# Attention scores of 16-bit batches: K's halves stacked over 128 rows, one head at a time

## The chip, the cores and the metric

The kernel runs on one core of one Trainium2 chip. A core has four compute engines with instruction streams of their own: TensorE (PE; its weight loads stand in the profile as PEld), VectorE (DVE), ScalarE (ACT) and GpSimd (POOL). SyncE (SP) issues the DMA transfers. The metric is device microseconds of one execution; before the change the median of three runs is 1104.53 us (1103.01 to 1106.8).

## What is computed

Eight batches, eight heads, 576 positions, head size 64: attention in a window of 128 positions with a linear bias, then a transform over positions and features, a norm and a two-layer network of width 2048.

```python
scores = scale * np.matmul(q, k.transpose(0, 1, 3, 2))
scores = np.where(mask, scores + bias[None], -1000000000.0)   # 0 <= rel < 128
attn = softmax(scores); attn_out = np.matmul(attn, v)
X = np.fft.fft(np.fft.fft(x, axis=1), axis=2); u = x + np.real(X)
un = (u - mean) / np.sqrt(var + 1e-06)
return u + np.maximum(un @ w_ch1, 0.0) @ w_ch2
```

## The kernel before, in words

**Pairs and tiles.** Two heads of a batch form a pair; pair p is batch p // 4 and heads 2j, 2j + 1 with j = p % 4. Q and K lie in memory with the head size over partitions, head 2j on partitions 0 to 63 and head 2j + 1 on 64 to 127. The queries of a head are cut into five tiles (`TILES`), four of 128 queries and one of 96; tile 0 sees 128 keys, the others 256. `SGRP` puts the tiles into three groups for the scores: (1, 0), (3, 2) and (4).

**Two kinds of batch.** Batches 0 to 2 (`NF = 3`) compute the scores in 32-bit numbers, one product per tile and head. Batches 3 to 7 split each 32-bit operand into a 16-bit high part and a 16-bit rest: `convert` (L331) makes the high part by an ACT copy (L353) and the rest by a DVE subtraction (L354, in the profile as L158). Q and K of a pair are converted whole, on 128 partitions, and V in the same way. `scores` (L362) then makes, for each tile and each head, three products over the 64 rows of that head: high by high, rest by high, high by rest (`prods`, L368), all added up in PSUM. The inner loop runs over the two heads, so that the products of the two heads alternate, each with its own PSUM tile, sp0 or sp1 (two buffers each).

**After the scores.** L390 reduces the scores with the bias and writes them to P; an exponential follows on ACT, then `halves` (L397) splits P into two 16-bit parts (ACT L403 and DVE), `flip` transposes them by DMA into pt (L412), and `values` (L428) multiplies them with V's two parts (L445 to L447). `weigh` (L451) divides by the sums and writes the batch's X.

**The rest of a batch.** `fourier` (L493) does the transform, `norm` (L647) the norm with transposes by DMA into uT, and `ffn` (L685) the two layers: L698 fills a PSUM tile fp with 24 products of 256 columns (or 48 of 128), ACT (L703) and DVE evacuate it into hbuf, and L712 makes the second layer from hbuf, 48 products of 512 columns per tile. Two PSUM buffers serve fp. Of the transform, 64 rows of every two batches are left over; they are gathered in a tile `ut` (L500, two buffers) and go through the network by themselves, with uT in a spare half of the second layer's weight tile (L653).

**What sets the order.** Every step is put into a heap with a time by hand (`put`), and the steps are emitted in the order of these times; from batch 1 on a batch has 24 units of time and a pair 6. A pair that starts at t loads Q and K at t - 7 (`load`, L301), converts Q at t - 4.6 and K at t - 3.6 (L733), makes the scores of its three groups at t, t + 2 and t + 4, both heads together (L736), and the value products at t + 5.66 to t + 10.66, head by head, one unit apart (L740). Loads, DMA transposes and outputs all go out from SP's queue, in order, and each waits there until its buffer is free. The framework then adds the semaphores and may move an instruction ahead on its engine when a modelled timeline has room for it. Buffers: one each for the raw Q (qr) and the raw K (kr), two each for the converted Q (qq) and K (kk).

`batch_scales` (L244) reads Q, K and V of a coming 16-bit batch through two slots (fetches at L253) and squares them on ACT (L257) to find the scales, among them `nsl`, whose columns 8 to 11 hold Q's scale by pair.

Of the kernel before, what the change touches and what calls it, by code (L numbers as in the profile page):

```python
# [76 lines left out]
def attn_fft_ffn_kernel(  # L77
# [30 lines left out]
    slope_sb = const.tile([128, 16], F32, name="slope_sb")  # L108
# [135 lines left out]
    def batch_scales(b, t0, dt):  # L244
# [19 lines left out]
        def scale():  # L264
# [8 lines left out]
            nsl = small.tile([128, 12], F32, name="nsl")  # L273
            V.tensor_scalar(nsl[:, 0:8], slope_sb[:, 0:8], gi[:, 0:1], None, ALU.mult)
            V.tensor_scalar(nsl[:, 8:12], slope_sb[:, 8:12], sc[:, 0:1], None, ALU.mult)
# [25 lines left out]
    def load(p):  # L301
        b, j = divmod(p, 4)
        qr = att.tile([128, NQ], F32, name="qr", bufs=1)
        if b < NF:
            kr = att.tile([128, 2, NQ], F16, name="kk").rearrange("p e t -> p (e t)").bitcast(F32)[:, 0:NK]
        else:
            kr = att.tile([128, NK], F32, name="kr", bufs=1)
        nc.sync.dma_start(out=qr, in_=q[b, j])
        nc.sync.dma_start(out=kr, in_=k[b, j])
        raws[p] = [qr, kr]  # L310

# [19 lines left out]
    def convert(p, what):  # L331
        b, j = divmod(p, 4)
        if b < NF:
            qr, kr = raws[p]
            qs = att.tile([128, 2, NQ], F16, name="qq").rearrange("p e t -> p (e t)").bitcast(F32)
# [4 lines left out]
        if what < 2:  # L340
            pair = att.tile([128, 2, NQ], F16, name="qk"[what] * 2)
            n, s = ((NQ, nsl[:, 8 + j:9 + j]), (NK, sc[:, 1:2]))[what]
            hi, lo, src = pair[:, 0, 0:n], pair[:, 1, 0:n], raws[p][what]
            ops.setdefault(p, []).extend((hi, lo))
        else:
# [6 lines left out]
            ops[p] += vh, vl  # L352
# [9 lines left out]
    def scores(p, i):  # L362
        b, j = divmod(p, 4)
        if b < NF:
            prods = ((ops[p][0], ops[p][1]),)
        else:
            qh, ql, kh, kl = ops[p][:4]
            prods = ((qh, kh), (ql, kh), (qh, kl))  # L368
        grp = SGRP[i]
        sp = [ps_s.tile([128, 512], F32, name=f"sp{e}") for e in range(2)]  # L370
        col = 0
        for ti in grp:
            c0, m, blks = TILES[ti]
            n = 128 * len(blks)
            for x, (qq, kk) in enumerate(prods):
                for e in range(2):
                    h = slice(64 * e, 64 * e + 64)
                    T.matmul(sp[e][:m, col:col + n], qq[h, c0:c0 + m], keys(kk[h], ti),  # L378
                             start=(x == 0), stop=(x == len(prods) - 1))
            col += n  # L380
        P = Ps[p, i] = {}
        for e in range(2):
# [45 lines left out]
    def values(p, i, e):  # L428
# [5 lines left out]
        for ti in TGRP[i]:  # L434
            m, blks = TILES[ti][1:]
            n = len(blks)
            for x, (vc, _) in enumerate(blks):
# [5 lines left out]
                vh, vl = ops[p][4:]  # L443
# [49 lines left out]
    def fourier(b, t0):  # L493
        st = {}

        def begin():
            XA = Xs[b]
            st["X"], st["X2"], st["sc"] = [XA[:, i] for i in XS], XA[:, 2], scs[b][0]
            if b % 2 == 0:
                uts[b // 2] = xp.tile([128, DM], F32, name="ut", bufs=2)  # L500
# [370 lines left out]
```

## Time and profile before

| | |
|---|---|
| runs | 1106.8, 1104.53, 1103.01 us |
| profiled execution | 1103.87 us |
| its span | 1102.1 us |
| mean granted clock of TensorE | 0.978 |
| PE / DVE / ACT busy | 1069.7 / 688.5 / 566.9 us |
| 16-bit score products (L378) | from 290.97 us (start of the first) to 899.24 us (last run of them) |

Busy times are sums over the whole span and say nothing of a stage. A row of a timeline gives the start, the length and, after an x, how many instructions stand in it. Matmuls are pipelined: the length of one is its latency, and the distance between two starts is the room that it takes. In a row of waits stand the total in us, the times and the longest. In a form such as `64*128 64x256 f16` the first product is rows by columns of the weights, the second partitions by columns of the data that stream through.

### The profile page before, as it was taken

The numbers are of one execution on the slowest core, as the hardware profiler recorded it, in microseconds if no ns is written. First come the engines' busy times: TensorE is split into PE (matmuls) and PEld (weight loads), VectorE is DVE, ScalarE is ACT, GpSimd is POOL, SyncE is SP. The second block draws the span as 40 slices with busy tenths as digits, with TensorE's granted clock in tenths as the row PEclk, the third lists the DMA queues.
The fourth block names the chain that finished last, engine by engine and source line by source line (L and its number), as shares of the span: only waits on it lengthen the run. The fifth ranks groups of instructions, "written<-read, shape, count | busy, mean of one in ns | idle before, by whom it ended". The sixth has DMA issues, their size and how long they took to land.

```text
span 1102.1 us, 23512 instructions
## 1 busy us (share of the span) xinstructions
PE 1069.7 (97%) x9220; PEld 754.4 (68%) x9220; DVE 688.5 (62%) x2023; ACT 566.9 (51%) x1333; POOL 20.1 (2%) x58
## 2 busy tenths in 40 slices
PE   6989999999888999999999999999999999999998
PEld 5777778686755666676667677585857676757665
DVE  6989678137456586868767585868685755262111
ACT  5867688448746565457534474456544441241000
POOL 0000000000000000000000000001000000010000
PEclk9989869999989999999999999999999999999999
DMA  9951245414656455344633144334531230030000
GB/s 368 321 191 57 66 109 162 129 35 104 200 155 146 131 100 109 76 102 83 129 80 85 42 106 100 86 81 105 119 86 37 56 81 1 20 53 16 20 10 20
DMA packets 170655, 109.61 MB, mean 99 GB/s; under 512 B 135472, under 2 KB 144944, under 8 KB 170544
## 3 DMA queue, kind: packets, MB, share of 16 engines
q1 hardware_dynamic: 169968, 106.66, 37.5%
q8 instruction: 72, 1.18, 0.4%
q10 hardware_dynamic: 576, 1.45, 0.3%
q14 instruction: 39, 0.32, 0.1%
HBM read 66.91 MB, written 9.44 MB: 69 GB/s over the span
## 4 chain that ended last, share of the span: by engine, by line
PE 83%; DMA 6%; DVE 5%; ACT 4%; issue 1%; SPq 0%; POOL 0%; ACTq 0%; DVEq 0%
PE fp L698 31%; PE fp L712 30%; PE sp L378 6%; PE pv L440 4%; PE pd L554 3%; DMA wall<-q_dram 2%; PE sp L421 2%; PE fp L299 2%; PE pd L588 1%; ACT wall L257 1%; DMA wall<-k_dram 1%; DMA vr<-v_dram 1%; PE pv L445 1%; ACT P L158 1%; PE pv L447 1%
## 5 line engine op out<-in xcount | busy, mean ns | idle before, releaser
L712 PE MATMUL fp<-wall,hbuf 128*128 128x512 f16 x1728 | 395.5, 381 | 2.9 <-DVE hbuf L158 2.9
L698 PEld LDWEIGHTS <-wall 128*128 128x128 f16 x3840 | 338.4, 98 | 53.2 <-issue 14.0
L698 PE MATMUL fp<-uT,wall 128*128 128x256 f16 x3072 | 361.1, 273 | 7.8 <-DVE hbuf L158 4.8
L712 PEld LDWEIGHTS <-hbuf 128*128 128x128 f16 x1728 | 163.3, 99 | 186.5 <-issue 10.0
L158 ACT ACTIVATE P<-P,nb 128x256 f32<-128x256 f32 x320 | 141.2, 478 | 117.3 <-DVE nb L390 117.2
L703 ACT ACTIVATE hbuf<-fp 128x512 f16<-128x512 f32 x144 | 85.0, 590 | 194.2 <-PE fp L698 194.2
L158 DVE SCALAR_TENSOR_TENSOR hbuf<-fp,hbuf 128x512 f16<-128x512 f32 x144 | 98.9, 688 | 136.1 <-ACT hbuf L703 135.5
L390 DVE CUSTOM_DVE_ANT_0 P<-sp,rg,nsl 128x256 f32<-128x256 f32 x200 | 80.5, 450 | 49.6 <-PE sp L378 49.5
L378 PE MATMUL sp<-kk,qq 64*128 64x256 f16 (+5 forms) x840 | 100.7, 310 | 6.8 <-DMA kk<-k_dram 5.4
L158 DVE SCALAR_TENSOR_TENSOR P<-P 128x256 f16<-128x256 f32 x200 | 73.5, 389 | 19.2 <-ACT P L403 17.9
L403 ACT ACTIVATE P<-P 128x256 f16<-128x256 f32 x200 | 70.9, 382 | 0.5 <-DMA pt<-P 0.3
L257 ACT ACTIVATE wall<-wall 128x512 f32<-128x512 f32 (+2 forms) x75 | 45.2, 604 | 48.1 <-DMA wall<-v_dram 20.3
L440 PEld LDWEIGHTS pv<-vr,pt 128*128 128x128 f32 x432 | 59.8, 213 | 4.6 <-issue 1.2
L440 PE MATMUL pv<-vr,pt 128*128 128x65 f32 x432 | 62.5, 294 | 0.2 <-DVE X L462 0.2
L158 DVE SCALAR_TENSOR_TENSOR X<-fp,misc,X 128x512 f32<-128x512 f32 x32 | 23.8, 743 | 56.3 <-PE fp L712 56.3
L390 DVE CUSTOM_DVE_ANT_0 P<-sp,rel_sb 128x256 f32<-128x256 f32 x120 | 42.1, 388 | 7.9 <-PE sp L378 7.9
L446 PE MATMUL pv<-vl,pt 128*128 128x64 f16 x360 | 46.4, 193 | 0.0
L447 PE MATMUL pv<-vhs,pt 128*128 128x65 f16 x360 | 46.3, 194 | 0.0
L445 PE MATMUL pv<-vhs,pt 128*128 128x65 f16 x360 | 45.9, 195 | 0.3 <-DVE X L462 0.3
L378 PEld LDWEIGHTS sp<-kk,qq 64*128 64x128 f32 (+1 forms) x240 | 31.9, 204 | 20.1 <-ACT qq L336 5.6
L698 PE MATMUL fp<-wall,wall 128*128 128x128 f16 x768 | 45.4, 219 | 0.1
L424 ACT ACTIVATE pt<-sp 128x384 f32<-128x384 f32 (+2 forms) x72 | 32.6, 464 | 15.7 <-PE sp L421 13.8
(146 smaller groups left out, 1197.7 us busy)
## 6 DMA issues: line engine op xcount, KB each, us to landing
qr<-q_dram SPq DMA_DIRECT2D x32, 304.0 KB, 3.0
hbuf<-w_dram SPq DMA_DIRECT2D x16, 512.0 KB, 6.7
out_dram<-X SPq DMA_DIRECT2D x32, 256.0 KB, 2.4
wall<-v_dram SPq DMA_DIRECT2D x25, 256.0 KB, 3.0
vr<-v_dram SPq DMA_DIRECT2D x20, 320.0 KB, 3.2
kr<-k_dram SPq DMA_DIRECT2D x20, 289.0 KB, 3.4
X<-w_dram SPq DMA_DIRECT2D x11, 512.0 KB, 5.3
wall<-q_dram SPq DMA_DIRECT2D x20, 256.0 KB, 2.8
```

The costliest lines, as they stand in the source:

```text
L158: put(now[0] + dt, lambda: f(*a, **kw))
L257: A.activation(t, t, AF.Square, accum_out=box["mx"][:, i, c:c + 1])
L378: T.matmul(sp[e][:m, col:col + n], qq[h, c0:c0 + m], keys(kk[h], ti), start=(x == 0), stop=(x == len(prods) - 1))
L390: V.tensor_tensor_reduce(pt[:m, 0:n], sp[e][:m, col:col + n], tab[:m, pc:pc + n], mul, 3.0e38, ALU.add, ALU.min, nb[:m, ti:ti + 1])
L403: A.activation(hi, P32, AF.Copy, scale=2.0 ** 14)
L440: T.matmul(pv[:, ti], pt[:, col:col + 128], ops[p][2][:, e, vc], start=first, stop=last)
L445: T.matmul(pv[:, ti], ph, vh[:, e, vc], start=first, stop=False)
L446: T.matmul(pv[:, ti, 0:D], ph, vl[:, e, vc], start=False, stop=False)
L447: T.matmul(pv[:, ti], pl, vh[:, e, vc], start=False, stop=last)
L698: T.matmul(fp[:, i * n:(i + 1) * n], w1_ap(e, c, f0 + i), uT[:, j, c, 0:n], start=(c == 0 and p == 0), stop=(c == 3 and p == 2))
L703: A.activation(ht[:, 0], fp, AF.Relu)
L712: T.matmul(op, hh[f][:, a, i * 128:(i + 1) * 128], w2_ap(e, f), start=(f == 0 and p == 0), stop=(f == 15 and p == 2))
```

## The change

In the 16-bit batches a head's scores no longer use its 64 rows of the array but all 128. K's high part and its rest are stacked over the partitions (head 0: high on 0 to 63 and rest on 64 to 127; head 1 the other way round), and Q of one head is loaded twice, onto both halves of the partitions. One product of Q's high part with the stack adds high by high and high by rest; a second one adds rest by high and rest by rest. So a tile takes two products per head, where there were three. The scores are made head by head: head 0 at t, t + 1, t + 2 and head 1 at t + 3, t + 4, t + 5.

Q is loaded and converted by head (loads at t - 7 and t - 4, conversions at t - 4.6 and t - 1.6), and K's two halves of 64 partitions are converted separately (t - 3.6 and t - 1.6). The pool of converted Q has three buffers, of which a pair takes two. To make room, `ut` has one buffer, and every second one of its tiles lies in the spare half of the second layer's weight tile. The table of slopes gets eight more columns, so that `nsl` holds Q's scale by head.

```diff
-            nsl = small.tile([128, 12], F32, name="nsl")
+            nsl = small.tile([128, 16], F32, name="nsl")
...
-            V.tensor_scalar(nsl[:, 8:12], slope_sb[:, 8:12], sc[:, 0:1], None, ALU.mult)
+            V.tensor_scalar(nsl[:, 8:16], slope_sb[:, 16:24], sc[:, 0:1], None, ALU.mult)
...
     def load(p):
         b, j = divmod(p, 4)
-        qr = att.tile([128, NQ], F32, name="qr", bufs=1)
         if b < NF:
+            qr = att.tile([128, NQ], F32, name="qr", bufs=1)
+            nc.sync.dma_start(out=qr, in_=q[b, j])
             kr = att.tile([128, 2, NQ], F16, name="kk").rearrange("p e t -> p (e t)").bitcast(F32)[:, 0:NK]
         else:
             kr = att.tile([128, NK], F32, name="kr", bufs=1)
-        nc.sync.dma_start(out=qr, in_=q[b, j])
+            qr = None
         nc.sync.dma_start(out=kr, in_=k[b, j])
         raws[p] = [qr, kr]
+
+    def load_q(p, e):
+        b, j = divmod(p, 4)
+        qr = raws[p][0] = att.tile([128, NQ], F32, name="qr", bufs=1)
+        nc.sync.dma_start(out=qr, in_=bass.AP(tensor=q.tensor, offset=q[b, j, 64 * e].offset,
+                                              ap=[[0, 2], [NQ, 64], [1, NQ]]))
...
-    def convert(p, what):
+    def convert(p, what, e=0):
...
-        if what < 2:
-            pair = att.tile([128, 2, NQ], F16, name="qk"[what] * 2)
-            n, s = ((NQ, nsl[:, 8 + j:9 + j]), (NK, sc[:, 1:2]))[what]
-            hi, lo, src = pair[:, 0, 0:n], pair[:, 1, 0:n], raws[p][what]
-            ops.setdefault(p, []).extend((hi, lo))
+        if what == 0:
+            s, src = nsl[:, 8 + 2 * j + e:9 + 2 * j + e], raws[p][0]
+            pair = ops.setdefault(p, {})["q", e] = att.tile([128, 2, NQ], F16, name="qq", bufs=3)
+            hi, lo = pair[:, 0], pair[:, 1]
+        elif what == 1:
+            if e == 0:
+                ops[p]["k"] = att.tile([128, 2, NQ], F16, name="kk")
+            own, other = slice(64 * e, 64 * e + 64), slice(64 - 64 * e, 128 - 64 * e)
+            s, src = sc[own, 1:2], raws[p][1][own]
+            hi, lo = (ops[p]["k"][x, e, 0:NK] for x in (own, other))
...
-    def scores(p, i):
+    def scores(p, i, heads=(0, 1)):
...
-        sp = [ps_s.tile([128, 512], F32, name=f"sp{e}") for e in range(2)]
+        sp = {e: ps_s.tile([128, 512], F32, name=f"sp{(e + (i if b >= NF else 0)) % 2}") for e in heads}
...
-            for x, (qq, kk) in enumerate(prods):
-                for e in range(2):
+            for e in heads:
+                if b < NF:
                     h = slice(64 * e, 64 * e + 64)
-                    T.matmul(sp[e][:m, col:col + n], qq[h, c0:c0 + m], keys(kk[h], ti),
-                             start=(x == 0), stop=(x == len(prods) - 1))
+                    T.matmul(sp[e][:m, col:col + n], ops[p][0][h, c0:c0 + m], keys(ops[p][1][h], ti),
+                             start=True, stop=True)
+                    continue
+                for x in range(2):
+                    T.matmul(sp[e][:m, col:col + n], ops[p]["q", e][:, x, c0:c0 + m], keys(ops[p]["k"][:, e], ti),
+                             start=(x == 0), stop=(x == 1))
...
-                uts[b // 2] = xp.tile([128, DM], F32, name="ut", bufs=2)
+                uts[b // 2] = wall[1][:, 8, 512:1024] if b // 2 % 2 else xp.tile([128, DM], F32, name="ut", bufs=1)
...
-            for what, x in enumerate((4.6, 3.6, -2 if early else 1.2)):
-                put(t - x, convert, p, what)
+            for e in range(2):
+                put(t + 3 * e - 7, load_q, p, e)
+                put(t + 3 * e - 4.6, convert, p, 0, e)
+                put(t + 2 * e - 3.6, convert, p, 1, e)
+            put(t - (-2 if early else 1.2), convert, p, 2)
         for i in range(3):
-            put(t + 2 * i * f, scores, p, i)
+            if b < NF:
+                put(t + 2 * i * f, scores, p, i)
+            else:
+                put(t + i, scores, p, i, (0, ))
+                put(t + i + 3, scores, p, i, (1, ))
```

More of the change, by code (lines that the diff above doesn't have):

```diff
@@ L107, in attn_fft_ffn_kernel @@
     rel_sb = const.tile([128, 1152], BF16, name="rel_sb")
-    slope_sb = const.tile([128, 16], F32, name="slope_sb")
+    slope_sb = const.tile([128, 24], F32, name="slope_sb")
     tab1_sb = const.tile([128, 4, 3, NS], F16, name="tab1_sb")
@@ L334, in convert @@
             qr, kr = raws[p]
-            qs = att.tile([128, 2, NQ], F16, name="qq").rearrange("p e t -> p (e t)").bitcast(F32)
+            qs = att.tile([128, 2, NQ], F16, name="qq", bufs=3).rearrange("p e t -> p (e t)").bitcast(F32)
             A.activation(qs, qr, AF.Copy, scale=slope_sb[:, 12 + j:13 + j])
@@ L351, in convert @@
             src = raws.pop(p)[2].rearrange("p a b c -> p (a b) c")
-            ops[p] += vh, vl
+            ops[p]["v"] = vh, vl
         A.activation(hi, src, AF.Copy, scale=s)
@@ L360, in keys @@
         return t[:, a0:a0 + 128 * len(TILES[ti][2])]
-    def scores(p, i):
+    def scores(p, i, heads=(0, 1)):
         b, j = divmod(p, 4)
[L364 to L368, printed above, removed]
         grp = SGRP[i]
-        sp = [ps_s.tile([128, 512], F32, name=f"sp{e}") for e in range(2)]
+        sp = {e: ps_s.tile([128, 512], F32, name=f"sp{(e + (i if b >= NF else 0)) % 2}") for e in heads}
         col = 0
@@ L374, in scores @@
             n = 128 * len(blks)
-            for x, (qq, kk) in enumerate(prods):
-                for e in range(2):
+            for e in heads:
+                if b < NF:
                     h = slice(64 * e, 64 * e + 64)
-                    T.matmul(sp[e][:m, col:col + n], qq[h, c0:c0 + m], keys(kk[h], ti),
-                             start=(x == 0), stop=(x == len(prods) - 1))
+                    T.matmul(sp[e][:m, col:col + n], ops[p][0][h, c0:c0 + m], keys(ops[p][1][h], ti),
[4 more added lines that the diff above has]
+                             start=(x == 0), stop=(x == 1))
             col += n
-        P = Ps[p, i] = {}
-        for e in range(2):
+        P = Ps.setdefault((p, i), {})
+        for e in heads:
             h = 2 * j + e
@@ L442, in values @@
                     continue
-                vh, vl = ops[p][4:]
+                vh, vl = ops[p]["v"]
                 ph, pl = (pt[:, o:o + 128] for o in (POUT[ti] + x * m, POUT[ti] + (n + x) * m))
@@ L778, in tables @@
     sl = 2.0 ** -(np.arange(8) + 1.0)
-    slope = np.zeros((128, 16), np.float32)
+    slope = np.zeros((128, 24), np.float32)
     slope[:, 0:8] = -sl
@@ L782, in tables @@
     slope[:, 12:16] = 0.125 * slope[:, 8:12]
+    slope[:, 16:24] = 1.0 / sl
     def split(t):
```

## The prediction

> **What bounds the kernel now.** I read the page first: the busy times and the chain.
>
> ```profile
> PE 1069.7 (97%) x9220; PEld 754.4 (68%) x9220; DVE 688.5 (62%) x2023; ACT 566.9 (51%) x1333; POOL 20.1 (2%) x58
> ...
> PE 83%; DMA 6%; DVE 5%; ACT 4%; issue 1%; SPq 0%; POOL 0%; ACTq 0%; DVEq 0%
> ```
>
> TensorE (PE) is busy for 97% of the span and holds 83% of the chain. The changed pairs (12 to 31) run from about 280 to 910 us, so I asked for busy times by stretch, and for what PE waited on between 290 and 910 us.
>
> ```profile
> 290.00:350.00 60.00, 52.81 (x404) 34.72 (x402) 35.57 (x106) 35.05 (x96) 0.21 (x2) 0.94 0.57 157
> 350.00:410.00 60.00, 56.69 (x587) 39.89 (x585) 37.23 (x108) 36.28 (x98) 0.90 (x3) 1.00 0.55 124
> 410.00:470.00 60.00, 60.00 (x580) 40.65 (x578) 44.61 (x136) 29.92 (x70) 0.80 (x2) 1.00 0.43 86
> ...
> 710.00:770.00 60.00, 60.00 (x570) 41.41 (x568) 45.74 (x144) 36.01 (x90) 2.95 (x5) 1.00 0.40 94
> ```
> ```profile
> PE fp L698 <- DVE hbuf L158: 3.8, 4, 1.7
> PE fp L698 <- DVE X L158: 3.0, 2, 2.4
> PE fp L712 <- DVE hbuf L158: 2.9, 1, 2.9
> PE pd L554 <- DVE zl L563: 1.5, 1, 1.5
> PE pv L445 <- DVE X L462: 0.3, 1, 0.3
> ```
>
> Columns after a stretch: its length, then busy time of PE, PEld, DVE (VectorE), ACT (ScalarE) and GpSimd, then granted clock and DMA. From 410 us on PE has no idle time that the trace shows, at full clock, with DVE near 75% and ACT at 50 to 60%. PE's waits, 11.5 us together, lie almost all ahead of 410 us: 7.2 us of idle time in the first stretch and 3.3 in the second. In the steady part a microsecond of PE work added or taken moves the end by as much.
>
> **Part one: the products.** The key rows are the groups by form (mean ns after the comma) and PE's timeline (start us, length, count).
>
> ```profile
> L698 PE MATMUL fp<-uT,wall 128*128 128x256 f16 x3072 | 361.1, 273 | 7.8 <-DVE hbuf L158 4.8 <-DVE X L158 3.0
> L378 PE MATMUL sp<-kk,qq 64*128 64x256 f16 x360 | 34.0, 274 | 0.0
> L378 PE MATMUL sp<-kk,qq 64*96 64x256 f16 x120 | 10.5, 271 | 0.0
> L378 PE MATMUL sp<-kk,qq 64*128 64x128 f16 x120 | 8.3, 217 | 0.0
> ```
> ```profile
> 290.97 0.67 PE L378 MATMUL sp<-kk,qq 64*128 64x256 f16 x12
> ...
> 305.94 2.79 PE L698 MATMUL fp<-uT,wall 128*128 128x256 f16 x24
> ...
> 641.69 0.19 PE L447 MATMUL pv<-vhs,pt 128*128 128x65 f16 x1
> 641.72 1.50 PE L698 MATMUL fp<-wall,wall 128*128 128x128 f16 x24
> 643.16 0.67 PE L378 MATMUL sp<-kk,qq 64*128 64x256 f16 x12
> ...
> 649.62 0.19 PE L446 MATMUL pv<-vl,pt 128*128 128x64 f16 x1
> 649.65 0.19 PE L447 MATMUL pv<-vhs,pt 128*128 128x65 f16 x1
> 649.77 0.83 PE L378 MATMUL sp<-kk,qq 64*128 64x256 f16 x12
> 650.54 0.68 PE L698 MATMUL fp<-wall,wall 128*128 128x128 f16 x9
> ...
> 899.24 0.51 PE L378 MATMUL sp<-kk,qq 64*128 64x256 f16 x6
> ```
>
> A mean of 274 ns is latency, not the room that a product takes. Room is the distance between starts. Full-height L698: (2.79 - 0.27)/23 = 0.110 us for 256 columns; (1.50 - 0.22)/23 = 0.056 for 128. The L378 run at 649.77 has twelve products of 256 columns. One after the other they would span 11 x 0.110 + 0.27 = 1.48 us; they span 0.83, and (0.83 - 0.27)/0.110 is 5.1 steps: six steps of two. So the two heads, on rows 0 to 63 and 64 to 127, already run at once, and "three products of 64 rows" are three steps for two heads, where the change needs four (two per head). Fewer instructions, 600 to 400, but more room.
>
> Against that stands the edge of each run. L447's starts are 0.03 apart, so after 649.65 the next start was due at 649.68; L378 comes at 649.77: 0.09 lost. Its last pair starts at 649.77 + 0.83 - 0.27 = 650.33 and takes 0.11, so L698 was due at 650.44 and comes at 650.54: 0.10 lost. Between two full-height kinds nothing is lost: 641.69 (L447) to 641.72 (L698) is the usual 0.03. So going between 64-row and 128-row products costs 0.19 us per run; the weight loads show the same edge as idle time ahead of L378, released by nothing (us in total, times, longest):
>
> ```profile
> PEld L378 <- issue: 18.3, 61, 0.4
> ```
> The instruction order cuts these products into 82 runs (the first and the last are quoted), 30 of them of odd count, where one product goes without a partner.
>
> Now: 600 products in (600 + 30)/2 = 315 steps, about 60 of them of 128 columns: 255 x 0.110 + 60 x 0.056 = 31.4 us; edges 82 x 0.19 = 15.6 us; together 47.0.
> Changed: 20 pairs x 2 heads x 5 tiles x 2 products = 400, a fifth with 128 columns: 320 x 0.110 + 80 x 0.056 = 39.7 us, and no edges if a full-height product beside L698 behaves as L447 does.
> Difference: -7.3 us of PE room. Bounds: with the edges kept at their present count, 39.7 - 31.4 = +8.3; if the pairs had not overlapped at all it would be (480 x 0.110 + 120 x 0.056) + 15.6 - 39.7 = -35.4, which the 0.83 us rules out. I take -7.3.
>
> The Trainium skill, "TensorEngine Tiling (Array Packing)", section "The Problem", counts a contraction of 64 or less as underuse that row tiling mends; by that alone the change is a loss, the +8.3. Its "Key Properties" says that changing the tiling mode drains TensorE, and here the trace agrees, at 0.09 and 0.10 us an edge; which of the two sentences is worth more is what the count of 82 decides.
>
> **Part two: the conversions.** Per pair, Q is converted once per head, and K in two halves of 64 partitions: four ACT copies and four DVE subtractions for two and two.
>
> ```profile
> L353 ACT ACTIVATE kk<-kr,sc x20: 761/762/777, 272.2 to 833.5; 128x578 f16<-128x578 f32 x20
> L353 ACT ACTIVATE qq<-qr,nsl x20: 785/796/804, 274.6 to 832.8; 128x608 f16<-128x608 f32 x20
> L158 DVE SCALAR_TENSOR_TENSOR kk<-kr,sc,kk x20: 809/815/822, 273.0 to 834.4; 128x578 f16<-128x578 f32 x20
> L158 DVE SCALAR_TENSOR_TENSOR qq<-qr,nsl,qq x20: 809/850/853, 275.4 to 833.6; 128x608 f16<-128x608 f32 x20
> ```
> ```profile
> L616 DVE TENSOR_TENSOR ut<-X,ds x8: 679/681/682, 141.6 to 977.3; 32x512 f32<-32x512 f32 x8
> ```
> ```profile
> L508 DVE TENSOR_TENSOR fg<-X x16: 671/673/681, 92.7 to 932.2; 128x512 f32<-128x512 f32 x16
> ```
>
> 32 partitions cost what 128 do (681 against 673 ns), so half of K costs a whole K: ACT gets 20 x (0.76 + 0.80) = +31 us, DVE 20 x (0.82 + 0.85) = +33 us. A batch (L616 runs once in each: (977.3 - 141.6)/7 = 119 us) gets for its four pairs 6.7 us more DVE work: about 75% becomes 80%. From 410 us on that is covered by PE's own work (60.00 of 60.00); with the cover gone it costs up to its own length. It is not covered where PE already waits for DVE:
>
> ```profile
> 283.00:313.00 30.00, 26.38 (x247) 22.57 (x245) 12.69 (x43) 17.63 (x49) 0.11 (x1) 1.00 0.58 171
> 340.00:375.00 35.00, 29.33 (x293) 24.05 (x292) 18.77 (x53) 21.85 (x60) 0.00 (x0) 1.00 0.62 159
> ```
>
> Up to 375 us three pairs' extra work falls: 3 x (1.56 + 1.67) = 9.7 us; between 0 and 9.7 of that can become PE wait. In these rows 70.9 us of DVE and ACT work stand beside 9.3 us of PE idle, a share of 0.13: I take +1.3 us. A gain is not excluded either: all 10.5 us of early idle could shrink if the order falls better.
>
> **Part three: Q's second load and the waits.** Each head's Q is loaded by itself, doubled over the partitions: two loads of 304 KB for one, through a single buffer, so a load must wait for the conversion before it. K's one buffer too is given back later, after its second half.
>
> ```profile
> SPq L308 <- DVE qq L158: 16.0, 10, 3.2
> ...
> SPq L309 <- DVE kk L158: 1.6, 5, 0.3
> ```
> ```profile
> qr<-q_dram SPq DMA_DIRECT2D x32, 304.0 KB, 3.0
> ```
> ```profile
> ACT qq L353 <- PE sp L378: 23.7, 10, 4.8
> ```
>
> A Q load already waits 1.6 us in ten of its cases; twenty more loads are 0 to 32 us more of waiting by SyncE's queue (SP), about 16 at the present rate of one in two. Behind a waiting load stand the transposes of P (L412), of uT, the outputs and the fetches for the scales (L253). The schedule keeps 2.4 units from load to conversion; a unit is 119/24 = 5.0 us, so some 12 us stand against 3.0 of landing. Covered; uncovered, a PE wait of the same length. Q's pool goes from two buffers to three, but two per pair are used: the margin from last use to reuse goes from 3.4 units to 2.4. ACT waits there already (23.7 us) while the list of PE's waits holds none for ACT; it may wait up to a unit, 5.0 us, longer each time, which I price at nothing, being followed by work that PE needs only units later.
>
> Head-by-head order gives back something: head 0's last scores run at t + 2 for t + 4, 5.7 units ahead of their value products instead of 3.7. PE's wait at L445 is only 0.3 us, so this is worth at most that. The number of score reductions, exponentials and transposes stays. The ut tile in the weights' spare half has the same writers and the same rotation of two: nothing. The wider scale is one instruction per batch as before, the slope table one load at the start: nothing.
>
> **Sum.** The profiled execution took 1103.87 us (span 1102.1), 0.7 below the median of 1104.53. 1103.87 - 7.3 + 1.3 = 1097.9, so 1098 us. I leave the 0.7 in the range.
>
> **Rivals.**
> 1. *The early waits eat it (slower).* Place: 283 to 375 us, where an evacuation that is late stops PE. Price: 9.7 us of extra conversions and three waits for Q of 1.6 (4.8), all as PE idle, and another half-clock stretch such as that behind the 0.94 (0.06 x 60 = 3.6): -7.3 + 18.1 = +10.8, 1115 us. For: PE waits on DVE there now. Against: the share is 0.13. It decides from 7.3 us on; half of the 18.1 gives 1106, no change that can be told.
> 2. *The edge is not the mode's.* If a change of line or bank costs the 0.19, head-by-head gives 120 runs: 120 x 0.19 = 22.8, and 39.7 + 22.8 - 47.0 = +15.5: 1119 us; kept at 82 it is +8.3: 1112. Against: L447 to L698 loses nothing. The sentence on underuse in the Trainium skill's "TensorEngine Tiling (Array Packing)", taken alone, leads to this 1112 too.
> 3. *The order falls better.* Early idle (10.5) and half clock (3.6) shrink by half: -7.3 - 7: 1090 us. For: scores come in smaller portions. Against: more conversions beside them.
> 4. *The change does less than it says.* The 96-column loads of tile 2 (up to 129 ns, below) may set the pace of its 80 products: 80 x (0.129 - 0.110) = 1.5 us; and a tenth to a fifth of the 33 us of extra DVE work may become PE wait in the steady stretch: 1103.87 - 7.3 + 1.5 + 3.3 to 6.6 = 1101 to 1105.
>
> ```profile
> L378 PEld LDWEIGHTS <-qq x600: 92/94/129, 291.0 to 899.4; 64*128 64x128 f16 x120, 64*96 64x96 f16 x30
> ```
>
> **How the numbers follow.** Forecast 0.55 (1094 to 1101), rival 3 0.13, rival 4 or half of rival 1 0.18, rival 1 in full 0.09, rival 2 0.05 (0.02 for 1119, 0.03 for 1112). What a measurement of this kernel can tell from no change is about 0.3%, 3.3 us: faster is below 1101.2, slower above 1107.8. So faster 0.68, same 0.18, slower 0.14. The range from 1090 to 1107 leaves out about 0.05 below and 0.15 above.
>
> **What would show it.** L378 at 16 bit as 400 products of full height, 0.110 apart, starting 0.03 to 0.11 after their neighbours; about 39 to 40 us of starts in place of 47; PEld's idle time of 0.3 us ahead of L378 gone; L353 and its subtractions doubled in count at the same length; PE's waits between 290 and 910 us near 11.5 us. Wrong would be: edges of 0.1 us still there, PE idle beyond 410 us, or DVE's hbuf releases above 15 us.

## The result, and the profile after

The changed kernel takes 1219.89 us (median of four runs, 1214.64 to 1222.6), the kernel before, on the same chip, 1104.37 (1103.01 to 1106.8). The ratio is 1.1038, 95% interval 1.1009 to 1.1066: slower by 115 us, where 6 us less were forecast. The profiled execution took 1220.61 us, with a span of 1218.8.

The page of the changed kernel: busy times, the slices of PE, granted clock and DMA, the main queue, the chain by engine, and the group of ACT's copies of Q.

```profile
PE 1097.9 (90%) x9020; PEld 785.7 (64%) x9020; DVE 720.0 (59%) x2063; ACT 602.0 (49%) x1373; POOL 18.2 (1%) x58
...
PE   6999998998687896989879997999679999999998
...
PEclk8987889999887998989889998999979999999999
DMA  9842164216486568687893468785995233002000
...
q1 hardware_dynamic: 172288, 112.88, 53.1%
...
PE 47%; DMA 22%; DVE 11%; ACT 5%; issue 3%; SPq 1%; DVEq 0%; ACTq 0%; POOL 0%
...
L365 ACT ACTIVATE qq<-qr,nsl 128x608 f16<-128x608 f32 x40 | 32.0, 799 | 107.2 <-DMA qr<-q_dram 88.7
```

PE is still the busiest engine, but it holds 47% of the chain where it held 83%, and DMA holds 22% where it held 6%. The same rows of the kernel before are `q1 hardware_dynamic: 169968, 106.66, 37.5%` and, for the slices, `DMA  9951245414656455344633144334531230030000`: 6% more bytes, and 53.1% of the engines' time for 37.5%. There are 1.4% more packets; what grew is the time that each held its engine. The last row is the first pointer: ACT waited 88.7 us for Q.

The idle time lies in the steady part, where there was none. The views of busy time by stretch, first before, then after (columns: length, busy time of PE, PEld, DVE, ACT, GpSimd, then granted clock, DMA share, GB/s):

```profile
290.00:410.00 120.00, 109.50 (x988) 74.61 (x986) 72.80 (x213) 71.33 (x194) 1.11 (x5) 0.97 0.56 140
410.00:1010.00 600.00, 598.92 (x5596) 415.16 (x5594) 402.74 (x1164) 287.42 (x675) 13.22 (x29) 1.00 0.35 76
```
```profile
290.00:410.00 120.00, 90.89 (x668) 66.29 (x667) 54.62 (x149) 62.75 (x158) 0.21 (x2) 0.86 0.65 142
410.00:1010.00 600.00, 534.91 (x4873) 378.93 (x4871) 406.16 (x1172) 307.32 (x701) 9.81 (x26) 0.95 0.70 84
```

From 410 to 1010 us PE is idle for 65 us instead of 1, the DMA engines are busy for 70% of the time instead of 35%, and they move 84 GB/s instead of 76. A tenth more data took double the time on the engines, so the packets stood there longer. PE's and DVE's waits in the changed kernel (total us, times, longest):

```profile
PE fp L709 <- DVE hbuf L158: 34.4, 10, 6.9
PE fp L709 <- DVE X L158: 11.2, 5, 4.8
PE pv L456 <- DVE X L473: 9.4, 3, 4.1
PE fp L709 <- DVE ut L158: 8.4, 1, 8.4
```
```profile
DVE qq L158 <- ACT qq L365: 64.6, 16, 8.1
...
DVE P L401 <- DMA pt<-P: 40.4, 9, 6.4
```

PE waits for evacuations by DVE that are late, and DVE stands, in order, behind Q's subtraction (64.6 us, through ACT's copy) and behind score reductions whose P tile a transpose has not yet left (40.4 us; 0 before). The chain of the changed kernel between 609 and 655 us (start, length, what) shows both in the place where they set the end:

```profile
609.87 8.70 DMA qr<-q_dram
618.57 0.02 issue
618.59 0.81 ACT qq L365
619.40 0.02 issue
619.42 0.85 DVE qq L158
...
622.51 0.03 issue
622.54 9.69 DMA pt<-P
...
634.14 8.77 DMA qr<-q_dram
...
644.65 8.53 DMA qr<-q_dram
```

A load of 304 KB that was forecast at 3.0 us takes 8.5 to 8.8, and a transpose of P next to it 9.69. From the trace's packet records (my count): the 128 packets of a Q load are of 2432 bytes and take 0.098 us at the median, before as after. In the median load of before, 11.1 of them are in flight and the last comes 2.5 us after the issue; after the change, 2.06 are in flight, and the last comes after 8.4 us. The 256-byte packets, those of the transposes, take 22 ns on average before and 37 after. Their median is 18 ns in both; what grew is the number of those that take over 1 us, from 103 to 596 of 123,904.

The products themselves did what was forecast. PE's timeline of the changed kernel, and the group of the full products:

```profile
449.48 0.19 PE L458 MATMUL pv<-vhs,pt 128*128 128x65 f16 x1
449.51 0.60 PE L389 MATMUL sp<-kk,qq 128*128 128x256 f16 x4
449.95 0.19 PE L456 MATMUL pv<-vhs,pt 128*128 128x65 f16 x1
```
```profile
L389 PE MATMUL sp<-kk,qq 128*128 128x256 f16 x240 | 46.5, 280 | 8.3 <-DVE nb L401 6.6 <-ACT qq L365 1.0 <-DVE qq L158 0.6
```

L389 starts 0.03 us after L458 and leaves the array free 0.44 later, 4 x 0.110: no edge at either end. Counted over all runs of the 16-bit score products, the median loss of a run in the kernel before is 0.095 us at its beginning and 0.092 at its end (82 runs); in the changed kernel (99 runs) and in e7 below (108) it is 0.00 at both.

Where the 115 us are: the span grew by 116.7. PE's idle time grew by 88.5 (1218.8 - 1097.9 against 1102.1 - 1069.7). Its busy time grew by 28.2, though e7 below, with the same products, is at 1061.0; the difference, 36.9, goes with a lower clock (0.938 for 0.978 on average; the clock records have half speed for 150.2 us, before for 47.8). In this trace the low clock goes with gaps in PE's work: each of the 17 records of half speed between 290 and 910 us has 1.9 to 5.4 us of PE idle time in the 10 us ahead of it, where 10 us between 300 and 1010 us hold 1.3 on average. So the longer busy time, too, goes with the waiting; no run changed the one without the other.

### The profile page after: what moved, and what is told of

Same layout as the page of the kernel before. It is cut to its first block, busy times and chain, and to the rows that moved or that the text cites. A ratio compares the mean times of both kernels' runs of the same rounds, so it can differ in the third digit from the quotient of the medians.

```text
span 1218.8 us, 23209 instructions
## 1 busy us (share of the span) xinstructions
PE 1097.9 (90%) x9020; PEld 785.7 (64%) x9020; DVE 720.0 (59%) x2063; ACT 602.0 (49%) x1373; POOL 18.2 (1%) x58
## 3 DMA queue, kind: packets, MB, share of 16 engines
q1 hardware_dynamic: 172288, 112.88, 53.1%
## 4 chain that ended last, share of the span: by engine, by line
PE 47%; DMA 22%; DVE 11%; ACT 5%; issue 3%; SPq 1%; DVEq 0%; ACTq 0%; POOL 0%
PE fp L709 20%; PE fp L723 19%; DMA qr<-q_dram 9%; DMA pt<-P 4%; DMA wall<-v_dram 3%; DMA wall<-k_dram 2%; PE pd L565 2%; DVE P L401 2%; ACT wall L257 1%; DVE P L158 1%; DVE qq L158 1%; PE sp L389 1%; PE pd L599 1%; DMA vr<-v_dram 1%; DMA uT<-un 1%
## 5 line engine op out<-in xcount | busy, mean ns | idle before, releaser
L709 PE MATMUL fp<-uT,wall 128*128 128x256 f16 x3072 | 388.1, 285 | 65.8 <-DVE hbuf L158 33.2
L158 ACT ACTIVATE P<-P,nb 128x256 f32<-128x256 f32 (+2 forms) x320 | 142.3, 480 | 117.6 <-DVE nb L401 116.9
L401 DVE CUSTOM_DVE_ANT_0 P<-sp,rg,nsl 128x256 f32<-128x256 f32 (+2 forms) x200 | 84.7, 449 | 64.5 <-DMA pt<-P 40.4
L158 DVE SCALAR_TENSOR_TENSOR P<-P 128x256 f16<-128x256 f32 (+2 forms) x200 | 73.5, 390 | 23.9 <-ACT P L414 23.5
L365 ACT ACTIVATE qq<-qr,nsl 128x608 f16<-128x608 f32 x40 | 32.0, 799 | 107.2 <-DMA qr<-q_dram 88.7
L158 DVE SCALAR_TENSOR_TENSOR qq<-qr,nsl,qq 128x608 f16<-128x608 f32 x40 | 33.9, 846 | 64.7 <-ACT qq L365 64.6
L414 ACT ACTIVATE P<-P 128x256 f16<-128x256 f32 (+2 forms) x200 | 70.7, 385 | 2.3 <-DMA pt<-P 1.2
L389 PE MATMUL sp<-kk,qq 128*128 128x256 f16 (+2 forms) x400 | 59.1, 270 | 8.3 <-DVE nb L401 6.6
L385 PE MATMUL sp<-kk,qq 64*128 64x256 f32 (+2 forms) x240 | 56.1, 429 | 7.0 <-DMA kk<-k_dram 5.3
L389 PEld LDWEIGHTS <-qq 128*128 128x128 f16 (+1 forms) x400 | 39.1, 107 | 19.7 <-issue 7.9
L401 DVE CUSTOM_DVE_ANT_0 P<-sp,rel_sb 128x256 f32<-128x256 f32 x120 | 42.4, 388 | 8.5 <-PE sp L385 8.2
L458 PE MATMUL pv<-vhs,pt 128*128 128x65 f16 x360 | 47.4, 195 | 0.0
```

Source lines behind the costliest of these rows:

```text
L158: put(now[0] + dt, lambda: f(*a, **kw))
L385: T.matmul(sp[e][:m, col:col + n], ops[p][0][h, c0:c0 + m], keys(ops[p][1][h], ti), start=True, stop=True)
L389: T.matmul(sp[e][:m, col:col + n], ops[p]["q", e][:, x, c0:c0 + m], keys(ops[p]["k"][:, e], ti), start=(x == 0), stop=(x == 1))
L401: V.tensor_tensor_reduce(pt[:m, 0:n], sp[e][:m, col:col + n], tab[:m, pc:pc + n], mul, 3.0e38, ALU.add, ALU.min, nb[:m, ti:ti + 1])
L414: A.activation(hi, P32, AF.Copy, scale=2.0 ** 14)
L458: T.matmul(pv[:, ti], pl, vh[:, e, vc], start=False, stop=last)
```

## The experiments

The runs came down to two theories. **A, waiting for Q:** the slow load through the single buffer qr delays the conversion, and DVE and ACT, which work in order, hold up everything behind it. **B, late neighbours:** a load on two engines keeps these two occupied, every other transfer has a share on them, and so transposes of P, K's loads and the scales' fetches all land late, whoever reads the slow load. The third possibility was that products, order or conversions had a cost of their own. The texts ahead of e1, e2, e4 and e5 use the letters otherwise: their A is all that the form of the load does (A and B here), their B is the doubled conversions with the single buffer, and their C is the order, head by head.

### Only the way in which Q arrives

**e1**: the changed kernel, each doubled load issued as two loads of 64 rows.

```diff
-        nc.sync.dma_start(out=qr, in_=bass.AP(tensor=q.tensor, offset=q[b, j, 64 * e].offset,
-                                              ap=[[0, 2], [NQ, 64], [1, NQ]]))
+        for h in (0, 64):
+            nc.sync.dma_start(out=qr[h:h + 64], in_=q[b, j, 64 * e:64 * e + 64])
```

> The changed kernel with each doubled Q load issued as two loads of 64 rows, one for each half of the partitions; all else as changed. Theory A (the load alone: its outermost dimension has size 2, so it uses 2 of the 16 DMA engines, lands after 7 us and more where a load of 128 rows takes 2.6, and holds up ACT and what is queued behind it): ACT's wait for qr falls from 88.7 us to under 10, the half-clock time from 150 us to about 50, and the time comes to the forecast, 1090 to 1107 us. Theory B (the doubled conversions and the single Q buffer that two heads must pass through are what stops PE; the loads only share in it): still over 1150 us. Theory C (the head-by-head order itself starves PE): still over 1150 us with no wait for qr.

Measured: 1111.71 us, ratio to before 1.0042 (1.0019 to 1.0064). ACT's wait for Q and the stretches of e1:

```profile
ACT qq L365 <- DMA qr<-q_dram: 11.1, 11, 2.6
```
```profile
290.00:410.00 120.00, 106.09 (x873) 74.83 (x874) 73.09 (x215) 76.57 (x200) 1.11 (x5) 0.97 0.55 152
410.00:1010.00 600.00, 590.51 (x5458) 426.03 (x5456) 433.37 (x1206) 318.13 (x710) 12.24 (x29) 1.00 0.39 86
```

The same bytes, 86 GB/s for 84, at a DMA share of 0.39 for 0.70. 108 of the 115 us are the form of that one access pattern. The time is a little above the 1090 to 1107 us expected, and the wait above the 10 us.

**e4**: one load again, but of 128 different rows, from an input in which each head's rows stand twice.

```diff
-        nc.sync.dma_start(out=qr, in_=bass.AP(tensor=q.tensor, offset=q[b, j, 64 * e].offset,
-                                              ap=[[0, 2], [NQ, 64], [1, NQ]]))
+        nc.sync.dma_start(out=qr, in_=qd[b - NF, 2 * j + e])
```

> The changed kernel with Q of the 16-bit batches held twice in an input of its own, so that a doubled Q is one load of 128 separate rows. Theory A: as with two loads of 64 rows, 1090 to 1107 us, perhaps 1 to 3 us less because SP issues 40 loads fewer. Theories B and C: over 1150 us.

Measured: 1110.27 us, 1.003 (1.0002 to 1.0057). So it is neither the count of loads nor their size.

**e2** and **e8**: the kernel before with Q's 16-bit loads in such a form, outermost size 2 (e2) and 4 (e8), 20 loads, same bytes.

```diff
-        nc.sync.dma_start(out=qr, in_=q[b, j])
+        if b < NF:
+            nc.sync.dma_start(out=qr, in_=q[b, j])
+        else:
+            nc.sync.dma_start(out=qr, in_=bass.AP(tensor=q.tensor, offset=q[b, j].offset,
+                                                  ap=[[0, 2], [NQ, 64], [1, NQ]]))   # e8: [0, 4], [NQ, 32]
```

In this cut and those of e14 and e18 the remarks behind # are not in the code.

> The kernel before with one edit: in the 16-bit batches a pair's Q is loaded in the changed kernel's form, 2 times 64 rows with a step of 0 (the first head's Q stands for both heads, the second head's Q is left out); products, conversions and order as before. Theory A: 20 such loads, each landing some 5 us later and holding up transposes on the same two engines: 1115 to 1160 us, and q1's share of the DMA engines well above 37.5% at fewer bytes read. Theories B and C: within 4 us of 1104, since nothing else of the change is in it.

> The kernel before with its 16-bit Q loads written as 4 times 32 rows with a step of 0 (the first 32 rows stand for all, the rest of Q is left out). If the size of the outermost dimension sets how many of the 16 DMA engines work, 128 packets of 0.098 us run on 4: about 3.1 us of data, 4.5 to landing, against 6.3 and 7.6 on 2 engines: a third or less of what the 2 times 64 form cost: 1104 to 1115 us. If any load with a step of 0 is slow by itself (repeated reads): like the 2 times 64 form, 1125 to 1145.

Measured: e2 1135.83 us, 1.0256 (1.0221 to 1.029); e8 1120.15, 1.0148 (1.0116 to 1.0181). In flight in the median load: 2.06 packets in e2, 3.97 in e8. The number follows the outermost size. e8 costs over half of what e2 does, where a third or less was expected. The landings of the neighbours (us from issue, last column), before and in e2:

```profile
vr<-v_dram SPq DMA_DIRECT2D x20, 320.0 KB, 3.2
kr<-k_dram SPq DMA_DIRECT2D x20, 289.0 KB, 3.4
...
wall<-k_dram SPq DMA_DIRECT2D x20, 256.0 KB, 2.9
...
pt<-P SPq DMA_TRANSPOSE x200, 2.4
```
```profile
vr<-v_dram SPq DMA_DIRECT2D x20, 320.0 KB, 5.2
kr<-k_dram SPq DMA_DIRECT2D x20, 289.0 KB, 6.1
...
wall<-k_dram SPq DMA_DIRECT2D x20, 256.0 KB, 5.6
...
pt<-P SPq DMA_TRANSPOSE x200, 3.1
```

In e8 K's loads land after 4.8 us and the transposes after 2.8. None of these transfers was touched. ACT waits for Q only 6.0 us in e2, in one case, and the time is still 28 us longer: theory A cannot be the whole. The loss of e2 lies between 290 and 410 us, where PE is busy for 89.82 of 120 us; from 410 to 1010 it is busy for 597.54 of 600. So twenty slow loads are absorbed in the steady part, and not in the first pairs.

The packet records show what holds the neighbours (my count, of the 20 K loads of the 16-bit batches, 128 packets each). In e2, 12 of the 20 have their first 112 packets started within 2.8 us, and the last 16, two sixteenths, only after 6.4 to 6.9 us, within 0.7 us of the end of the Q load ahead of them. In e8 it is the last 32, four sixteenths, in 10 of the 20, after 3.5 to 4.8 us. In the kernel before, in e1 and in e4 no K load has such a gap; in the changed kernel 14 have it, with 16 packets. So the slow load holds up that share of the others that lies on its own engines, and the rest of each load passes it: the queue as a whole does not stand. One K load of the changed kernel has 123 of its packets late, which this does not explain.

### Does it need anyone to wait for the slow load?

**e12**: the changed kernel with two buffers for qr, so that a load can start earlier (room from one of the nine P buffers and one of the six pt buffers).

```diff
-PB = 9
+PB = 8
...
-        qr = raws[p][0] = att.tile([128, NQ], F32, name="qr", bufs=1)
+        qr = raws[p][0] = att.tile([128, NQ], F32, name="qr", bufs=2)
...
-            pts[p, i, e] = att.tile([128, 448], F32, name="pt", bufs=6).bitcast(F16)
+            pts[p, i, e] = att.tile([128, 448], F32, name="pt", bufs=5).bitcast(F16)
```

> The changed kernel, its doubled loads on two DMA engines as they are, with a second buffer for raw Q (room for it from P, 8 buffers for 9, and pt, 5 for 6). If most of the 108 us comes from the chain through the single buffer (load of 8.4 us, conversion, next load, while ACT stands in its order behind it), ACT's wait for qr falls below 45 us and the time to 1130 to 1175. If it comes from the other transfers that queue behind the loads on the same two engines: 1200 or more.

Measured: 1214.6 us, 1.1015 (1.0965 to 1.1066). Between 410 and 1010 us ACT's wait for Q fell from 67.0 to 16.8 us, and nothing was won. A wait of PE, and the groups of DVE and ACT that now wait for transposes (last figures: idle time, and what ended most of it):

```profile
PE pv L456 <- DMA pt<-P: 13.3, 3, 6.6
```
```profile
L401 DVE CUSTOM_DVE_ANT_0 P<-sp,rg,nsl 128x256 f32<-128x256 f32 (+2 forms) x200 | 84.6, 449 | 67.3 <-DMA pt<-P 48.4
...
L414 ACT ACTIVATE P<-P 128x256 f16<-128x256 f32 (+2 forms) x200 | 71.7, 386 | 31.2 <-DMA pt<-P 29.9
```

Most of the wait for Q is gone and the time is the same, now spent in waits for transposes (91.6 us in these three rows, 41.6 in the changed kernel). That speaks against theory A in its simple form, with a reservation: the smaller pools can lengthen these waits by themselves. L401 needs a P buffer that a transpose has left, and there are eight for nine; with five pt buffers the transposes wait longer on SyncE for PE to give one back (57.8 us for 26.9). No run has the smaller pools with the load mended, so e12 alone does not price the two.

**e14, e13, e15**: the kernel before plus loads that nobody reads, into a spare half of the second layer's weight tile: 20 in the two-engine form (e14), 40 of them (e13), 40 with the same bytes in the 128-row form (e15). A small VectorE instruction ahead of each paces it.

```diff
+    def load_spare(p, x):
+        b, j = divmod(p, 4)
+        to, seen = wall[1][:, 8, 512:1024], ops[p][5][:, 0, 0, 0:1] if x else ops[p][3][:, 0:1]
+        V.tensor_scalar(to[:, 0:1], seen, 1.0, None, ALU.mult)
+        nc.sync.dma_start(out=to, in_=bass.AP(tensor=q.tensor, offset=q[b, j].offset,
+                                              ap=[[0, 2], [NQ, 64], [1, 512]]))   # e15: in_=q[b, j, :, 0:512]
...
+            put(t + -3, load_spare, p, 0)
+            put(t + 2.6, load_spare, p, 1)      # not in e14
```

> As the one before with 20 such loads, one per pair. Contention: 1115 to 1140 us, like the 1135.8 of 20 folded Q loads. The wait for Q: 1104 to 1108.

> The kernel before, complete, with 40 more loads of 2 times 64 rows of 512 columns (256 KB each, 64 packets of 0.084 us on each of two engines, 5.4 us) into a spare place that nothing reads, two per 16-bit pair, each behind one small DVE instruction that sets its time. Nobody waits for them. If the other transfers queue behind them (theory: contention on two engines): landing of the transposes and of K's loads grows as in the kernel with 20 folded Q loads and beyond, and the time comes to 1130 to 1200 us. If the cost lies in the wait for Q itself: 1104 to 1112 (40 small instructions of about 0.2 us).

> The control: 40 loads of the same bytes in the form of 128 rows, on 16 engines, with the same small instructions. Both theories: 1104 to 1112 us, landing of the transposes near 2.4 us.

Measured: e14 1127.98 us, 1.021 (1.018 to 1.024); e13 1205.91, 1.0931 (1.0891 to 1.0971); e15 1114.56, 1.0096 (1.0066 to 1.0125). e14 is the clean one: no instruction of the computation reads these loads, VectorE's pacing instruction waits 0.3 us in all, SyncE never waits at one for an earlier one, and 23 us are lost, about as many as in e2. The packet gap is there too: in 5 of the 20 K loads the last 16 of 128 packets are late, in 9 of the 20 V loads the last 32 of 256. The bytes are not the cost, as 40 plain loads add only 0.4% (e17, below). That is theory B alone. Its place is that of e2:

```profile
290.00:410.00 120.00, 94.51 (x768) 65.74 (x766) 56.72 (x167) 63.00 (x174) 0.21 (x2) 0.90 0.64 140
410.00:1010.00 600.00, 597.97 (x5665) 412.30 (x5664) 418.42 (x1231) 296.31 (x700) 14.48 (x32) 1.00 0.52 85
```

e13 had a flaw of mine: its pacing instruction waited itself on VectorE for the load before (125.8 us in 19 cases), and e15's too (37.7).

**e16, e17, e18** mend that: e16 is e13 and e17 is e15 with the pacing on GpSimd, and e18 is e16 with the second load of a pair at t + 0.

```diff
-        V.tensor_scalar(to[:, 0:1], seen, 1.0, None, ALU.mult)
+        G.tensor_copy(to[:, 0:1], seen)
...
-            put(t + 2.6, load_spare, p, 1)      # e18 alone; seen is Q's or K's rest there
+            put(t + 0, load_spare, p, 1)
```

> The kernel before plus 40 loads of Q in the doubled form (outermost size 2, step 0) that nobody reads, each paced by a small instruction on GpSimd instead of VectorE. If late neighbours on the two engines' queues are the cost, the 20 such loads that cost 24 us already say what 40 cost at least: 1135 to 1200 us, with P's transposes landing in 2.8 us or more instead of 2.4, K's fetches in 5 us or more instead of 3.4, and the queue's share over 45%. If the cost of the 40 loads in the run before was VectorE's own wait of 125.8 us for them, nothing of it is left here and the time is that of the kernel before plus the control's addition: 1104 to 1118 us.

> The control: the same 40 unread loads with the same bytes and the same pacing on GpSimd, in the form of 128 different rows. Both theories: 1103 to 1112 us, P's transposes at 2.4 us. If this one is slow as well, it is the added bytes or the added instructions, and not the two engines, that cost the time.

> As the 40 unread two-engine loads paced by GpSimd, but each pair's second one 2.6 units earlier (t + 0 in place of t + 2.6), so that two loads stand 15 us apart and SyncE has no earlier one to wait for: its wait at that line should fall from 109.4 us to under 20. If the late neighbours are the cost, 1140 us or more remain (twice the 24 us of the 20 loads, or more, as the queues fill), with P's transposes, V and K landing late as before. If SyncE's own waiting behind such a load was the cost, what is left is what 20 such loads cost without it: 1120 to 1135 us.

Measured: e16 1194.01 us, 1.0818 (1.0783 to 1.0853), where one of its four runs took 2724.94 us, which nothing here explains, and the other three 1190 to 1194; e17 1108.42, 1.0038 (1.0016 to 1.0059); e18 1169.66, 1.0604 (1.0574 to 1.0635). With 117.14 MB on the queue in both, e16's form costs 86 us more than e17's, though of the engines only GpSimd, which paces them, waits for these loads, and the others wait for GpSimd no longer than before (3.1 us, before 3.5). What e16 waits for, and its SyncE queue (both of e16), then SyncE in e18:

```profile
ACT P L410 <- DMA pt<-P: 50.4, 12, 6.2
```
```profile
SPq L335 <- DMA wall<-q_dram: 109.4, 17, 7.6
```
```profile
SPq L335 <- DMA wall<-q_dram: 83.5, 19, 7.6
```

The first row is theory B. The second is another thing that a slow load does: it makes the queue's next load into the same buffer wait, with all that stands behind it. In e18 that wait should have fallen under 20 us and fell to 83.5, so e18 does not separate the two for 40 loads. 24 us of time went with 25.9 us of that wait, which leaves room for it to carry a good part. In both, PE loses time in the steady part as well: from 410 to 1010 us it is busy for 564.13 us in e16 and 576.21 in e18, for 599.04 in e17. In the changed kernel this wait is 32.7 us (L316), and without it, in e12, the time was the same.

### The products, the order and the conversions by themselves

**e7**: the changed products in the changed order, with the loads and conversions of before (both heads share one stacked pair of operands).

```diff
+        nc.sync.dma_start(out=qr, in_=q[b, j])
...
+            pair = ops.setdefault(p, {})["q", 0] = att.tile([128, 2, NQ], F16, name="qq", bufs=3)
+            ops[p]["q", 1] = pair
...
+            hi, lo = (ops[p]["k"][:, x, 0:NK] for x in range(2))
```

> The changed kernel's 128-row products and order, with the loads and conversions of before: Q is loaded once per pair and converted once, K converted once on all partitions, and both heads use the same operands (so the second head's own data and the stacking are left out). It prices what is left over after the load is mended, 1111.7 us. If the doubled conversions are what keeps that kernel from the forecast: 1104.7 - 7.3 = 1097 us (1095 to 1100) with PE's waits back near before's 33 us. If the head-by-head order does it: 1108 to 1112.

Measured: 1102.77 us, 0.9976 (0.9956 to 0.9997). PE is busy for 1061.0 us, 8.7 less than before, and idle for 40.1 where it was 32.4: of the room that the products give back, 7.7 us turn into waiting. Its stretch from 410 us:

```profile
410.00:1010.00 600.00, 595.33 (x5488) 430.98 (x5485) 406.37 (x1172) 293.39 (x675) 11.74 (x29) 1.00 0.36 77
```

PE had 1.1 us of idle time there, now 4.7, and e1 has 9.5. The ratios of e7 and e1 differ by 0.66%, 7 us: that is what the doubled conversions and the further loads (80 of 64 rows for 20 of 128) cost together.

**e5**: the products of 64 rows of before, in the changed order, head by head.

> The kernel before, its loads, conversions and 64-row products unchanged, but the scores made head by head in the changed kernel's order (head 0 at t, t + 1, t + 2, head 1 at t + 3 to t + 5), so that most products have no partner on the other 64 rows. If the two heads' products overlap in pairs before and each run costs 0.19 us at its edges: 480 x 0.110 + 120 x 0.056 = 59.5 us of products and 118 runs x 0.19 = 22.4 us take the place of 31.4 and 15.6: +35, 1140 us (1130 to 1150). Without overlap: +7 for the edges alone, 1111. If the order by itself starves PE (theory C), PE's waits grow beyond before's 33 us as well.

Measured: 1131.99 us, 1.0249 (1.0219 to 1.028), PE busy 31.8 us longer. One row of e5's timeline, to be laid beside the prediction's run at 649.77 (0.83 us for twelve products):

```profile
646.44 0.83 PE L378 MATMUL sp<-kk,qq 64*128 64x256 f16 x6
```

Six products of one head take as long as twelve of two. The overlap of the two row halves, on which part one rested, is shown.

**e3**: before, with the three products of head 0 issued first and then those of head 1.

```diff
-            for x, (qq, kk) in enumerate(prods):
-                for e in range(2):
+            for e in range(2):
+                for x, (qq, kk) in enumerate(prods):
```

> The kernel before with the loops over heads and products exchanged, so that the three 64-row products of one head follow each other and the two heads no longer alternate. If the two heads' products overlap in pairs now, 480 x 0.110 + 120 x 0.056 = 59.5 us of room takes the place of 31.4: 1104 + 28 = 1132 us (1120 to 1140). If they don't overlap, no change (1101 to 1108). The edges of 0.19 us stay in both.

Measured: 1109.5 us, 1.0037 (1.0018 to 1.0057); the expected loss of the overlap did not come. By its text that would mean that nothing overlaps, which e5 rules out; its runs keep their length:

```profile
437.54 0.51 PE L378 MATMUL sp<-kk,qq 64*128 64x256 f16 x6
```

**e6**: before, with the scores' groups 0 and 1 both at t, for fewer runs (53 for 82).

> The kernel before with the scores of groups 0 and 1 put at the same time (t, t, t + 4 in place of t, t + 2, t + 4): 53 runs of 64-row products in place of 82, nothing else. If an edge pair costs 0.19 us: 29 x 0.19 = -5.5 us, and fewer products without a partner (-0.5): 1098 to 1100 us. If the edges cost nothing, or the earlier scores crowd DVE and ACT: 1104 or more.

Measured: 1108.84 us, 1.0035 (1.0012 to 1.0058). By the count of its runs (53) the products' room fell by some 6 us. Its profiled execution, at 1114.93 us the slowest of twelve, has 42.2 us of PE idle time for 32.4 and half speed for 62.4 us for 47.8, so the gain was lost again there.

**e9, e10, e11** tried to get the change's own gain out: e4 with K's rest made on GpSimd; e4 with both heads at t, t + 2 and t + 4; and e7 with both heads so.

```diff
+        if what == 1:
+            after(0.3, G.tensor_scalar, src, src, s, None, ALU.mult)
+            after(0.35, G.tensor_tensor, lo, src, hi, ALU.subtract)
+            return
```

> The kernel with Q's rows doubled in an input (1110.3 us), with the rest of K (40 subtractions of 0.82 us) moved from DVE to GpSimd, in two steps there. If DVE's extra conversions are what keeps that kernel above 1102.8 (the time with one conversion): DVE falls back to about 687 us and the time to 1100 to 1106. If the extra loads or ACT's copies do it, or GpSimd's steps come late for the scores: 1108 or more.

> The kernel with Q's rows doubled in an input, but both heads' scores made together at t, t + 2, t + 4 as before (Q of the second head loaded and converted 0.3 units earlier). If the head-by-head order costs PE the 6 to 8 us of waits that remained with one conversion: 1102 to 1105. If the order costs nothing: 1110 as without it.

> 128-row products with the loads, the conversions and the order of before (both heads use the same operands, so the second head's own data and the stacking are left out): nothing of the change but the products. If the order cost the 6 us that separate 1102.8 from the forecast: 1095 to 1098. If the waits come from something else (the way the freed PE time falls): 1101 to 1104.

Measured: e9 1112.9 us, 1.0084 (1.0059 to 1.0109); e10 1114.02, 1.0081 (1.0052 to 1.0111); e11 1108.18, 1.0043 (1.0021 to 1.0065). None helps. In e9 DVE's busy time falls to 709.3 us and not to the 687 expected. The order of the change is better for its products than the old one (e7 against e11). No version that computes the whole beats the kernel before.

## Why the prediction was wrong

**The step that failed is part three**, where the load was priced "12 us stand against 3.0 of landing. Covered". The 3.0 us came from the row of a load of 128 different rows, and the change's load has another access pattern, `[[0, 2], [NQ, 64], [1, NQ]]`. It runs on two engines (2.06 packets in flight) and takes 8.4 us. 8.4 is still under 12, so by the prediction's own test it would have passed as covered. The 12 us were not there either: half of the 40 conversions began less than 10 us after the issue of their load (my count), and ACT waited 88.7 us for Q. And the test was too narrow: it asked when the load's reader needs it, not what the load does to the others on the same engines. e14 shows that share with no reader at all.

Step by step, as ratios to the kernel before: products and order 0.9976 (e7); with the doubled conversions and loads 1.0042 (e1); with the access pattern as well 1.1038. In microseconds of 1104 the steps are -2.6, +7.3 and +110.

**Part one** was right in mechanism and room: edges gone, starts 0.110 apart, 400 products, PE's busy time 8.7 us down where 7.3 were forecast. Mis-sized is what becomes of it: 7.7 us come back as idle time, and 1 to 3 us of gain remain. PE's full busy time from 410 us on was taken for a bound in both directions. Work added to PE does move the end (e5: 31.8 us of it, 28 of time), but work taken away does not by as much, as DVE follows close behind: the first layer's products wait 13.9 us for DVE in e7 and 7.8 before.

**Part two**: count and length were right, in the changed kernel's groups:

```profile
L365 ACT ACTIVATE kk<-kr,sc 64x578 f16<-64x578 f32 x40 | 30.8, 769 | 0.5
...
L158 DVE SCALAR_TENSOR_TENSOR kk<-kr,sc,kk 64x578 f16<-64x578 f32 x40 | 32.7, 817 | 2.9 <-ACT kk L365 1.7
```

The cost, with the loads', is about 7 us and not 1.3: they were not covered in the steady part either (1.1 us idle before, 4.7 in e7, 9.5 in e1). Rival 4's "a tenth to a fifth of the 33 us" is nearest to that.

**The rivals.** Rival 1 had the right sign and place of the wait, late hbuf evacuations, and a tenth of the size (+10.8 for +115), and it put them ahead of 375 us. Rival 2 is ruled out by L389's starts, over all of its runs. No rival asked whether the new load is carried like the old one.

The Trainium skill, "DMA: Bandwidth & Descriptors", has the rule, in the paragraph on how many engines of "Why a DMA increments its semaphore by 16 and not by 1": a transfer goes to the largest number of engines, up to sixteen, that divides the size of the slowest dimension that isn't of size 1, on both of its sides, so that an outermost size of two leaves two. The traces agree (2.06 in flight for size 2, 3.97 for 4, 11.1 for 128 rows). It also says that on the path of SyncE's transfers these are the lowest-numbered engines; no run here shows which they are. What such a load costs the others, e2 and e14 show.

**What stays open.** Forty two-engine loads cost 86 us (e16), twenty cost 23 (e14). How the difference divides between still later neighbours and SyncE's waits behind a slow load was not settled, as e18 took only a quarter of those waits away. So theory B is shown to suffice for the first 23 to 28 us, which lie ahead of 410 us. Most of the changed kernel's loss lies behind: 64 us more of PE idle time from 410 to 1010 us, where twenty slow loads (e2, e14) cost 1 to 2 and only forty cost more (e16: 36 idle, e18: 24). That part is late neighbours, the wait for Q and SyncE's waits together. e12 took most of the wait for Q away and won nothing, but with smaller pools, so the split of the changed kernel's 110 us stays open.

## What to carry to other kernels

Read a changed DMA's access pattern, not only its bytes: an outermost size of 2 puts 304 KB on two engines, 8.4 us for 2.5, and issuing it as two loads of 64 rows won back 108 of 115 us. When a load is called covered, ask who else has packets on the engines that it occupies; the first sign in the profile is the DMA share against GB/s (0.70 at 84 for 0.35 at 76). And before counting a saving of PE room as time, look at how much slack the engines behind PE have: here 7.7 of 8.7 us came back as idle time.

## What the runs showed of the hardware that was not expected

- Products of the two row halves overlap also when three of one half are issued ahead of three of the other (e3: 0.51 us for six, where e5's one half takes 0.83). It looks as if each half took its products on its own within a run. The trace does not record the order in which they were issued; that the starts of a pair lie mostly 10 ns apart in e3, and 3 to 4 in the kernel before, speaks for the order as written. No run tested that further.
- Subtracting K's rest on GpSimd takes two steps of 2542 and 1407 ns for 64x578 numbers (e9), against 817 ns for one step on DVE; and other work of DVE took longer beside it: its half of P's split 421 ns, in e4 389.
- A load on two engines holds up two sixteenths of the next loads' packets until it has ended, a load on four engines four sixteenths, and lets the others pass (e2, e8).
- Transfers that nobody reads and that move the same bytes cost 0.4% or 8.2% of the kernel's time by their access pattern alone (e17, e16).
